# Loading the second feature tile's raw weights earlier and the first stored queries later in a fused linear-attention and gated-MLP layer

## The chip, the cores and the metric

The kernel runs on one core of one Trainium2 chip. The metric is the device time of one execution in microseconds (us). A profiled execution has a span (first to last instruction on the core) and, a little longer, its own time; both are given below.

## The reference

The layer normalises x (2048 tokens, 512 features) and runs two branches on the result.

```python
qkv = (xn @ wqkv) -> q, k, v                      # 32 heads of 16
pq, pk = q @ w_phi, k @ w_phi                     # per head
phi(p) = concat(softmax(p), softmax(-p))          # 32 features per head
kv = sum_s phi_k[s]^T v[s];  z = sum_s phi_k[s]
o  = (phi_q @ kv) / (phi_q . z + 1e-6)
s  = o @ wo
h  = relu(xn @ W_gate) * (xn @ W_up)              # 1376 features
g  = silu(h @ W_down)
out = x + s * g
```

All of it is float32.

## The kernel before, in words

**Arithmetic.** Every large float32 product is made of three matmuls on parts: a value is split into a high part, rounded on ScalarE (ACT), and a low part, the difference, on VectorE (DVE) or GpSimd (POOL). `mm3` (lines 204 to 213) issues low x high, high x low and high x high. Projections and the gate and up products use a seven-product scheme on two-by-two blocks (Strassen's kind): the token blocks and their sums lie in one resident tile `XT`, the weight blocks and their sums are prepared per tile of 128 features.

**Stages.** First come eight pairs of token tiles: normalise, transpose, project k and v, form the features `ek`, add their products with v into one accumulator `pkv`, and store the projected queries to DRAM (`pq...`). One column pair of the later queries is made by `q_tile` (lines 640 to 686) in the seven-product form, after the pairs. Then the feature tiles f = 0 to 10 run for the first half of the tokens, `gate_up_apart` (lines 757 to 805) while no down-projection is pending and `gate_up` afterwards, with `down` between them; then the output rows of that half; then the same for the second half with weights reloaded from DRAM.

**The first feature tiles.** `gate_up_apart` makes seven blocks of six matmuls in this order: pa (weights `wa`), pb and pc (`wb`), pd (`wc`), pa again (`wa`), pc again (`wc`), pd again (`wd`). Between them DVE combines the results: `u <- pb, t` (t is ACT's copy of pa, line 763), `e <- pc, u`, `e <- pd, e`, and so on. The second block on pc adds into the buffer that `e <- pc, u` reads, and the second block on pd adds into the buffer that `e <- pd, e` reads. So each of those two blocks waits for that DVE instruction.

**Preparation of a feature tile.** `f_load` (lines 535 to 544) issues three loads of 256 KB from SyncE's (SP's) queue: two halves of the raw gate and up weights, `rawg`, and the raw down weights, `rawd`. `f_prep` (lines 557 to 614) turns them into `wa`, `wb`, `wc`, `wd` and `fdh`, `fdl`: POOL forms the sums `tab`, ACT rounds, POOL subtracts, and each part is stored to DRAM (`ws...`) for the second half. At its end it calls `f_load` for the next tile (lines 607 to 612). The three raw tiles come from a pool of 40 buffers of 2 KB per partition, so a load waits until the earlier user of its buffer is done.

**State and queries.** `state` (lines 1426 to 1441) issues the last products into `pkv`, copies them (ACT, `kvacc`), transposes them (DVE, `kvT`) and copies the result into `kvt` (DVE, four copies). `normalizers` (lines 1443 to 1462) loads the second feature sum, `zodd`, for which SP waits until POOL's last accumulating transfer has landed. `q_load(u)` (lines 851 to 856) loads two stored query parts, `pql`. `q_pair(u)` (lines 858 to 952) transposes them on DVE (`pq <- pql`), takes the largest and smallest value per head (`mx`, two reductions), and shifts and exponentiates (`eq`).

**What sets the order.** Every engine runs its instructions in the order in which they are issued. A small clock model in the kernel (`Clock`, lines 68 to 161) holds generators such as `f_prep` and `q_pair`, each yielding the tiles that it wants next. At every `pump` the model decides by its own estimates whether a generator's next step is issued at that place. So a line that is moved can change the place of other steps too. Line 64 records every instruction, which is why all rows of the profile name it.

Of the kernel before, what the change touches and what calls it, by code (L numbers as in the profile page):

```python
# [20 lines left out]
NF = -(-F // P)  # L21
# [143 lines left out]
def layer_kernel(ctx: ExitStack, tc: tile.TileContext, x, wkT, wqT, wv, wo, wf, cst, out):  # L165
# [9 lines left out]
    def u8(shape, name, dt=F32):  # L175
        return sb.tile(list(shape), dt, tag="u8", bufs=B8, name=name)

    def u4(shape, name, dt=F32):
        return sb.tile(list(shape), dt, tag="u4", bufs=B4, name=name)

    def u2(shape, name, dt=F32):
        return sb.tile(list(shape), dt, tag="u2", bufs=B2, name=name)

    def small(n, name, bufs=3):
        return sb.tile([P, n], F32, tag=name, bufs=bufs, name=name)
# [4 lines left out]
    def f32(t):  # L190
        return t.bitcast(F32)

    def add(engine, o, a, b, op=ALU.add):
        engine.tensor_tensor(o, a, b, op=op)
# [23 lines left out]
    def flat(e):  # L218
        return e.rearrange("p h s f -> p (h s f)")
# [201 lines left out]
    def query(n):  # L421


        h, d = divmod(n, 4)
        if d // 2 in Q_TILES[h // 2]:
            return
        c = slice(h % 2 * 2 * P, (h % 2 + 1) * 2 * P)

        qs = [2 * b + h % 2 for b in PAIRS[h // 2][::-1]]
        p = ps((P, 2, 2 * P), name="pq")  # L430

        def w_of(d):
            return wq_part(d // 2, d % 2)
        if n < 2:
            i = 1 - n
            for d in range(2):
                mm3(p[:, d, :], w_of(d), lambda k: [XT[:, 2 * i + k // 2, s, k % 2, c] for s in range(2)], range(KD),
                    d == 0)
            to = [((qs[i], 0), slice(None), slice(None))]
        else:  # L440
            mm3(p, w_of(d), lambda k: [XT[:, k // 2:k // 2 + 3:2, s, k % 2, c] for s in range(2)], range(KD))
            to = [((q, d // 2), d % 2, i) for i, q in enumerate(qs)]
        t = u2((P, 2, 2 * P), "pqs")
        nc.scalar.activation(t, p, AF.Copy)
        for q, col, part in to:
            put_q(q, col, t, t[:, part, :])
# [78 lines left out]
    RAW, FT, WD = {}, {}, {}  # L525

    def two(name, apart):
        if apart:
            return [u2((P, 2, 2, P), name) for c in range(2)]
        t = u4((P, 2, 2, 2, P), name)  # L530
        return [t[:, c] for c in range(2)]
# [3 lines left out]
    def f_load(f):  # L535
        if f in AHEAD:

            t = u8((P, 2, 2, 2, 2, P), "rawg")
            RAW[f] = [t[:, 0, c] for c in range(2)], u2((P, D), "rawd"), [t[:, 1, c] for c in range(2)]
        else:  # L540
            RAW[f] = two("rawg", True), u2((P, D), "rawd"), None
        for c in range(2):
            nc.sync.dma_start(RAW[f][0][c].rearrange("p k s f -> p (k s f)"), wf[f][:, c * 512:(c + 1) * 512])
        nc.sync.dma_start(RAW[f][1], wf[f][:, 1024:])

    def w_pair(name):
        return u2((P, 2, 2, P), name, F32R), u2((P, 2, 2, P), name, F32R)
# [3 lines left out]
    def flat3(t):  # L551
        return t.rearrange("p a b c -> p (a b c)") if len(t.shape) > 2 else t

    def put(f, i, t):
        pace.when(t, lambda: nc.sync.dma_start(wspill[f][i], f32(flat3(t))))

    def f_prep(f, keep=True):


        rg, rd, tab = RAW.pop(f)  # L560
        b11, b12, b21, b22 = (rg[c][:, :, s, :] for c in range(2) for s in range(2))
        ta, tb = tab or two("tab", True)
        yield "gpsimd", b22
        add(nc.gpsimd, tb[:, 0], b12, b11, ALU.subtract)
        add(nc.gpsimd, ta[:, 1], b22, b12, ALU.subtract)
        if keep:
            wa, wb = w_pair("wa"), None
        else:
            t = u8((P, 4, 2, 2, P), "wab", F32R)
            wa, wb = (t[:, 0], t[:, 1]), (t[:, 2], t[:, 3])  # L570
        yield "scalar", b11
        for c in range(2):
            nc.scalar.activation(wa[0][:, c], rg[c][:, :, 0, :], AF.Copy)
        put(f, 0, wa[0])
        yield "gpsimd", ta
        add(nc.gpsimd, ta[:, 0], b22, tb[:, 0], ALU.subtract)
        add(nc.gpsimd, tb[:, 1], b21, ta[:, 0], ALU.subtract)
        wb = wb or w_pair("wb")
        yield "scalar", ta
        nc.scalar.activation(wb[0], ta, AF.Copy)  # L580
        put(f, 2, wb[0])
        for c in range(2):
            yield from sums_of(wa[1][:, c], rg[c][:, :, 0, :], f32(wa[0][:, c]), ALU.subtract, wa[0])
        put(f, 1, wa[1])
        wc = w_pair("wc")
        yield "scalar", tb
        nc.scalar.activation(wc[0], tb, AF.Copy)
        put(f, 4, wc[0])
        yield from sums_of(wb[1], ta, f32(wb[0]), ALU.subtract, wb[0])
        put(f, 3, wb[1])  # L590
        wd = u2((P, 2, 2, P), "wd", F32R)
        yield "scalar", b22
        nc.scalar.activation(wd[:, 0], b22, AF.Copy)
        yield from sums_of(wc[1], tb, f32(wc[0]), ALU.subtract, wc[0])
        put(f, 5, wc[1])
        fd = u2((P, D), "fdh", F32R), u2((P, D), "fdl", F32R)
        yield "scalar", rd
        nc.scalar.activation(fd[0], rd, AF.Copy)
        put(f, 7, fd[0])
        yield "gpsimd", wd  # L600
        add(nc.gpsimd, wd[:, 1], b22, f32(wd[:, 0]), ALU.subtract)
        put(f, 6, wd)
        yield from sums_of(fd[1], rd, f32(fd[0]), ALU.subtract, fd[0])
        put(f, 8, fd[1])
        if keep:
            FT[f], WD[f] = [wa, wb, wc, wd], fd
            nxt = f + 1
            while nxt in AHEAD:
                nxt += 1
            del rg, rd, ta, tb, tab  # L610
            if nxt < NF:
                f_load(nxt)
        DONE.add(f)
        yield None,
# [236 lines left out]
    def q_load(u):  # L851
        for j, part in enumerate(UNITS[u]):
            PQS[2 * u + j] = u2((P, 2, 2 * P), "pql")
            for g in PUT_Q.pop(part):
                pace.finish(g)
            nc.sync.dma_start(PQS[2 * u + j], PQ[part])
# [306 lines left out]
    def sums_of(o, a, b, op=ALU.subtract, *need):  # L1163

        yield "gpsimd", *(need or (a, b))
        add(nc.gpsimd, o, a, b, op)
# [252 lines left out]
    nc.vector.memset(ones, 1.0)  # L1419
    kvt = sb.tile([P, NG, 32], F32, tag="kvt", bufs=1, name="kvt")  # L1420
    nc.vector.memset(kvt, 0.0)
    q_load(0)
    query(N - 1)
    pace.pump()

# [17 lines left out]
    def normalizers():  # L1443
        nonlocal zB, zacc, zodd
        yield "sync", zacc2
        zodd = u4((P, H, 2, DH), "zodd")
        nc.sync.dma_start(flat(zodd), zacc2)
        yield 64,
        yield "tensor", zacc, zodd
        for part in (zacc, zodd):  # L1450
            z = flat(part).rearrange("p (a d i x) -> p i a d x", a=2, d=4, i=4)
            for i in range(4):
                r = slice(32 * i, 32 * i + 32)
                nc.tensor.matmul(PKV[0][r, 4:].rearrange("p (a b) (d x) -> p a (b d) x", a=2, x=32), ones, z[:, i],
                                 start=False, stop=True, skip_group_check=True, tile_position=(0, 32 * i))
        part = z = zacc = zodd = None
        t = small(256, "zB", 1).rearrange("p (d x) -> p d x", d=4)
        nc.scalar.activation(t.rearrange("p d (a x) -> p a d x", a=2),
                             PKV[0][:, 4:].rearrange("p (a b) (d x) -> p a (b d) x", a=2, x=32), AF.Copy)
        zB = t  # L1460
        PKV.clear()
        yield None,

    def all_queries(half):
        nonlocal zs
        if not half:
            yield from state()
            zs = pace.add(normalizers(), first=True)
            yield 24,
        for u, parts in enumerate(UNITS):  # L1470
            if parts[0][0] in QUERIES[half]:
                if u > 3:
                    yield "limit", (1.5, 1)
                yield from q_pair(u)
# [24 lines left out]
    for half in range(2):  # L1499
        b0, b1 = 2 * half, 2 * half + 1  # L1500
        if half == 0:
            queries = pace.add(all_queries(0), 30)
            at[0] = N
            for q in Q_TILES[1]:
                for _ in q_tile(1, q):
                    pace.pump()
# [126 lines left out]
```

## Time and profile before

| | before |
|---|---|
| time, median of 3 runs | 546.84 us (546.66 to 548.46) |
| the profiled execution's own time | 546.74 us |
| its span | 545.0 us, so 1.74 us lie around it |
| busy: PE (TensorE matmul) / PEld (its weight load) | 539.6 / 440.5 us |
| busy: DVE / ACT / POOL | 372.4 / 258.7 / 366.9 us |
| moved by DMA | 125.98 MB, mean 231 GB/s |

How to read the lines that follow. A row of the timeline gives the start in us from the span's start, the time taken, the engine, the line, the operation with its tiles (out <- in, buffer numbers left out), the shape and the count. Brackets give the idle time of that engine just before the row, and what seems to have ended it. A row on PEld shows a gap of TensorE that the PE row, whose ends are modelled, hides. A row of the windows gives the length of a stretch, then the busy time of each engine with its instruction count, the granted clock of TensorE as a share of full speed, the mean busy share of the 16 DMA engines and GB/s.

### The profile page before, as it was taken

How to read it: one execution, taken by the hardware profiler on the slowest of the kernel's cores; microseconds unless marked ns; L12 is line 12 of the kernel's file. 1: busy time of each engine (PE TensorE's matmuls, PEld its weight loads, DVE VectorE, ACT ScalarE, POOL GpSimd, SP SyncE). 2: the span in 40 equal slices, each digit the busy share in tenths (PEclk: the TensorE clock that was granted, in tenths of full speed). 3: DMA queues.
4: the chain of work that ended last, by engine and by line, in shares of the span. 5: the costliest groups of instructions: out<-in, count | busy, mean ns of one | idle time of the engine just before them, and what ended most of it. 6: DMA issues, size and time to landing. Idle time of an engine off the chain costs nothing.

```text
span 545.0 us, 9140 instructions
## 1 busy us (share of the span) xinstructions
PE 539.6 (99%) x3186; PEld 440.5 (81%) x3186; DVE 372.4 (68%) x585; ACT 258.7 (47%) x462; POOL 366.9 (67%) x328
## 2 busy tenths in 40 slices
PE   9999999999999999999999999999999999999997
PEld 8898888877887888787887888887777887878886
DVE  5988778677768338789883442899999494924323
ACT  3788767654435564545434240334354545342510
POOL 1569999767787999899896235262365765842591
PEclk9999999999999999999999999999999999999999
DMA  8339789555899957887869998692664735657073
GB/s 283 147 129 326 177 215 237 133 131 107 197 284 391 334 179 275 301 298 272 289 242 337 412 414 313 240 366 73 223 200 135 275 112 166 221 186 277 0 233 115
DMA packets 76367, 125.98 MB, mean 231 GB/s; under 512 B 6689, under 2 KB 29089, under 8 KB 75425
## 3 DMA queue, kind: packets, MB, share of 16 engines
q1 hardware_dynamic: 74160, 117.99, 61.7%
q0 software_dynamic: 2016, 7.34, 7.7%
q8 instruction: 25, 0.41, 0.3%
q14 instruction: 22, 0.17, 0.1%
q10 hardware_dynamic: 144, 0.07, 0.0%
HBM read 68.49 MB, written 52.69 MB: 222 GB/s over the span
## 4 chain that ended last, share of the span: by engine, by line
PE 90%; DVE 6%; issue 1%; DMA 1%; POOL 1%; ACT 0%; DVEq 0%; POOLq 0%; ACTq 0%
PE py L64 20%; PE pd L64 10%; PE pa L64 10%; PE pk L64 9%; PE pb L64 9%; PE pso L64 8%; PE pc L64 6%; PE pq L64 6%; PE pv L64 5%; PE pkv L64 2%; PE pfold L64 1%; PE pnum L64 1%; PE pxT L64 1%; DVE qs L64 1%; DMA wb<-ws 1%
## 5 line engine op out<-in xcount | busy, mean ns | idle before, releaser
L64 PE MATMUL py<-fdh,hl 128*128 128x512 f32 x176 | 69.1, 392 | 0.0
L64 PE MATMUL py<-fdl,hh 128*128 128x512 f32 x176 | 68.5, 389 | 0.0
L64 PE MATMUL py<-fdh,hh 128*128 128x512 f32 x176 | 68.5, 389 | 0.0
L64 PE MATMUL pa<-XT,wa 128*128 128x512 f32 x264 | 67.3, 390 | 0.0
L64 PEld LDWEIGHTS pa<-XT,wa 128*128 128x128 f32 x264 | 49.4, 188 | 11.1 <-POOL tab L64 0.4
L64 DVE TENSOR_TENSOR y<-py,y 128x512 f32<-128x512 f32 x40 | 27.5, 689 | 31.4 <-PE py L64 31.3
L64 POOL TENSOR_TENSOR hl<-t,hh 128x512 fp32r<-128x512 f32 x16 | 20.7, 1295 | 39.5 <-ACT hh L64 39.5
L64 POOL TENSOR_TENSOR y<-y,ys 128x512 f32<-128x512 f32 x24 | 30.9, 1292 | 17.9 <-ACT ys L64 17.4
L64 PEld LDWEIGHTS py<-fdh,hl 128*128 128x128 f32 x176 | 33.0, 188 | 8.8 <-issue 1.2
L64 PEld LDWEIGHTS py<-fdh,hh 128*128 128x128 f32 x176 | 33.0, 188 | 6.9
L64 POOL TENSOR_TENSOR ez<-eq,zB 128x1024 f32<-128x1024 f32 x16 | 38.5, 2412 | 0.1
L64 PEld LDWEIGHTS py<-fdl,hh 128*128 128x128 f32 x176 | 33.0, 188 | 6.7
L64 PE MATMUL pd<-XT,wd 128*128 128x512 f32 x132 | 33.9, 392 | 0.2
L64 PE MATMUL pd<-XT,wc 128*128 128x512 f32 x132 | 33.9, 391 | 0.0
L64 PE MATMUL pb<-XT,wb 128*128 128x512 f32 x132 | 33.6, 390 | 0.0
L64 POOL TENSOR_TENSOR ol<-of,oh 128x512 fp32r<-128x512 f32 (+1 forms) x13 | 19.8, 1548 | 20.3 <-ACT oh L64 20.3
L64 ACT ACTIVATE hh<-t 128x512 fp32r<-128x512 f32 x16 | 10.1, 633 | 49.3 <-DVE t L64 48.1
L64 PE MATMUL pc<-XT,wb 128*128 128x512 f32 x132 | 33.5, 389 | 0.0
L64 DVE TENSOR_REDUCE mx<-pk 128x32 f32<-128x512 f32 x32 | 20.5, 683 | 16.6 <-PE pk L64 16.5
L64 PE MATMUL pq<-XT,wqh 128*128 128x512 f32 (+1 forms) x112 | 30.6, 360 | 0.0
L64 DVE TENSOR_TENSOR pb<-pb,t 128x512 f32<-128x512 f32 x16 | 11.1, 696 | 28.4 <-ACT pd L64 28.3
L64 PE MATMUL pk<-wkh,XT 128*128 128x512 f32 x88 | 30.3, 396 | 0.0
(203 smaller groups left out, 1456.6 us busy)
## 6 DMA issues: line engine op xcount, KB each, us to landing
xts<-XT SPq DMA_DIRECT2D x4, 1792.0 KB
zacc<-ek POOLq DMA_DIRECT2D x14, 512.0 KB, 5.5
XT<-xts SPq DMA_DIRECT2D x7, 1024.0 KB
rawg<-wf SPq DMA_DIRECT2D x22, 256.0 KB
ws<-wa SPq DMA_DIRECT2D x22, 256.0 KB
ws<-wb SPq DMA_DIRECT2D x22, 256.0 KB
ws<-wc SPq DMA_DIRECT2D x22, 256.0 KB
wa<-ws SPq DMA_DIRECT2D x22, 256.0 KB
```

What stands on the lines that cost most here:

```text
L64: return self.tc.keep_in_program_order(op(*a, **k))
```

## The change

Three edits.

1. In `f_prep`, tile 0 calls `f_load(1)` right after its first two `wa` copies, where preparation begins, and no longer at its end.
2. At the end of `f_prep` the next tile is loaded only if it has not been loaded.
3. `q_load(0)`, the load of the first two stored query parts, moves from before the last query projection to `all_queries`, behind `state()` and the start of `normalizers`.

```diff
         for c in range(2):
             nc.scalar.activation(wa[0][:, c], rg[c][:, :, 0, :], AF.Copy)
         put(f, 0, wa[0])
+        if f == 0:
+            f_load(1)
         yield "gpsimd", ta
...
-            if nxt < NF:
+            if nxt < NF and nxt not in RAW:
                 f_load(nxt)
...
     nc.vector.memset(kvt, 0.0)
-    q_load(0)
     query(N - 1)
...
             yield from state()
             zs = pace.add(normalizers(), first=True)
+            q_load(0)
             yield 24,
```

**SP, from the end of the pairs to the first feature tile.** The piece below is of the difference (minus: before, plus: after). `pql` are the first query parts, `rawg` and `rawd` the raw weights of tile 1, `ws_..._71` to `_75` stores of tile 0's parts, `ws_0_77` the first store of tile 1's.

```order
+L64 DMA ws_3_71<-wb 128x512
+L64 DMA ws_7_75<-fdh 128x512
+L64 DMA ws_5_73<-wc 128x512
+L64 DMA ws_0_77<-wa 128x512
 L64 DMA pql<-pq_1414 128x512
 L64 DMA pql<-pq_1731 128x512
-L64 DMA ws_3_71<-wb 128x512
-L64 DMA ws_7_75<-fdh 128x512
-L64 DMA rawg<-wf 128x512 x2
-L64 DMA rawd<-wf 128x512
-L64 DMA ws_5_73<-wc 128x512
 L64 DMA ws_6_74<-wd 128x512
```

The query loads now stand behind four stores, the last of which belongs to tile 1. The loads of tile 1 are gone from here: they now directly follow the loads of tile 0, ahead of a store of projected queries (`pq_1730 <- pqs`).

**ACT, from the q tile to the first block of tile 0.** `t_1912` and `t_2058` (before) are the copies of pa in the q tile and in tile 0; `wa`, `wb`, `wc`, `wd`, `fdh` here are tile 1's. Before:

```order
L64 ACTIVATE t_1912<-pa 128x512 x2
L64 ACTIVATE wa<-rawg 128x256 x2
L64 ACTIVATE kvacc<-pkv 128x256
L64 ACTIVATE wb<-tab 128x512
L64 ACTIVATE wc<-tab 128x512
L64 ACTIVATE wd<-rawg 128x256
L64 ACTIVATE fdh<-rawd 128x512
L64 ACTIVATE t_2058<-pa 128x512
```

After:

```order
L64 ACTIVATE t_1914<-pa 128x512
L64 ACTIVATE wa<-rawg 128x256 x2
L64 ACTIVATE t_1914<-pa 128x512
L64 ACTIVATE kvacc<-pkv 128x256
L64 ACTIVATE wb<-tab 128x512
L64 ACTIVATE wc<-tab 128x512
L64 ACTIVATE wd<-rawg 128x256
L64 ACTIVATE fdh<-rawd 128x512
L64 ACTIVATE t_2058<-pa 128x512
```

The two `wa` copies of tile 1, which need the raw weights, moved ahead of the second copy of the q tile; what follows `kvacc` stands as it did.

**DVE, from the end of the q tile to the first queries.** `u_1923`, `e_1942`, `t_2015` are the q tile's sums, `u_2078` and `e_2092` those of feature tile 0, `pq_2095` and `mx` the first query part. Before:

```order
L64 TENSOR_TENSOR t_2015<-pc,u_1923 128x512
L64 STREAM_TRANSPOSE kvT<-kvacc 128x256
L64 COPY kvt<-kvT 32x8x16 x4
L64 TENSOR_TENSOR u_1923<-pd,u_1923 128x512
L64 TENSOR_TENSOR u_2078<-pb,t_2058 128x512
L64 TENSOR_TENSOR e_2092<-pc,u_2078 128x512
L64 STREAM_TRANSPOSE pq_2095<-pql 128x512
L64 TENSOR_REDUCE mx<-pq_2095 128x32 x2
L64 TENSOR_TENSOR e_2092<-pd,e_2092 128x512
```

After:

```order
L64 STREAM_TRANSPOSE kvT<-kvacc 128x256
L64 COPY kvt<-kvT 32x8x16 x4
L64 TENSOR_TENSOR t_2022<-pc,u_1925 128x512
L64 TENSOR_TENSOR u_1925<-pd,u_1925 128x512
L64 TENSOR_TENSOR u_2078<-pb,t_2058 128x512
L64 STREAM_TRANSPOSE pq_2088<-pql 128x512
L64 TENSOR_REDUCE mx<-pq_2088 128x32 x2
L64 TENSOR_TENSOR e_2098<-pc,u_2078 128x512
L64 TENSOR_TENSOR e_2098<-pd,e_2098 128x512
```

Two things moved: the state's transpose and copies went ahead of one sum of the q tile, and the first query's transpose and reductions went ahead of `e <- pc, u` of tile 0. The order on PE is the same in both kernels, and POOL's too.

## The prediction

> **What bounds the kernel now.** I read the page first, then TensorE's gaps on its weight loads, then what each gap waited for.
>
> ```profile
> span 545.0 us, 9140 instructions
> PE 539.6 (99%) x3186; PEld 440.5 (81%) x3186; DVE 372.4 (68%) x585; ACT 258.7 (47%) x462; POOL 366.9 (67%) x328
> PEclk9999999999999999999999999999999999999999
> PE 90%; DVE 6%; issue 1%; DMA 1%; POOL 1%; ACT 0%; DVEq 0%; POOLq 0%; ACTq 0%
> ```
>
> TensorE (PE) is busy for 99% of the span at full clock, and 90% of the chain that ended last is its own work. The change leaves its 3186 matmuls in their order. So the only time to be had, or lost, lies in PE's waits. In the stretch that the change touches, from 130 us to 185 us, the weight loads show two gaps that are not part of a fixed sequence and that the moved steps can reach:
>
> ```profile
> 162.10 1.32 PEld L64 LDWEIGHTS pc<-XT,wc 128*128 128x128 f32 x6
> 163.84 1.22 PEld L64 LDWEIGHTS pd<-XT,wd 128*128 128x128 f32 x6 [0.43 <-POOL fdl L64]
> ...
> 179.63 0.19 PEld L64 LDWEIGHTS py<-fdh,hl 128*128 128x128 f32 x1 [0.35 <-POOL hl L64]
> ```
>
> The matmul rows around them give what each gap cost:
>
> ```profile
> 160.96 1.52 PE L64 MATMUL pa<-XT,wa 128*128 128x512 f32 x6
> 162.32 1.52 PE L64 MATMUL pc<-XT,wc 128*128 128x512 f32 x6
> 163.88 1.63 PE L64 MATMUL pd<-XT,wd 128*128 128x512 f32 x6
> 165.34 0.85 PE L64 MATMUL pa<-XT,wa 128*128 128x512 f32 x3
> ...
> 178.86 0.39 PE L64 MATMUL py<-fdh,hl 128*128 128x512 f32 x1
> ...
> 180.43 1.54 PE L64 MATMUL pb<-XT,wb 128*128 128x512 f32 x6
> ```
>
> Blocks of six start 162.32 - 160.96 = 1.36 us apart. After pc at 162.32 the pa block should start at 162.32 + 2 x 1.36 = 165.04; it starts at 165.34. **Gap 1 costs 0.30 us.** After py at 178.86 the next block should start at 180.22; it starts at 180.43. **Gap 2 costs 0.21 us.** Together 0.51 us, or 0.09% of the time.
>
> **What gap 1 waited for.** The row names POOL's fdl, but pd's second block adds into the buffer that DVE's `e <- pd, e` reads.
>
> ```profile
> 157.70 0.69 DVE L64 TENSOR_TENSOR u<-pd,u 128x512 f32<-128x512 f32 x1
> 159.69 0.69 DVE L64 TENSOR_TENSOR u<-pb,t 128x512 f32<-128x512 f32 x1 [1.29 <-ACT t L64]
> 160.48 0.69 DVE L64 TENSOR_TENSOR e<-pc,u 128x512 f32<-128x512 f32 x1
> 161.09 0.72 DVE L64 STREAM_TRANSPOSE pq<-pql 128x512 f32<-128x512 f32 x1
> 161.84 1.29 DVE L64 TENSOR_REDUCE mx<-pq 128x32 f32<-128x512 f32 x2
> 163.05 0.68 DVE L64 TENSOR_TENSOR e<-pd,e 128x512 f32<-128x512 f32 x1
> ```
>
> It ends at 163.05 + 0.68 = 163.73, and the load starts 0.11 us later. It was late because the chain began late: `u <- pb, t` waited 1.29 us for ACT's t.
>
> ```profile
> 154.68 0.42 ACT L64 ACTIVATE wa<-rawg 128x256 fp32r<-128x256 f32 x1 [2.33 <-DMA rawg<-wf]
> 155.59 0.37 ACT L64 ACTIVATE kvacc<-pkv 128x256 f32<-128x256 f32 x1
> 156.84 0.63 ACT L64 ACTIVATE wb<-tab 128x512 fp32r<-128x512 f32 x1 [0.88 <-POOL tab L64]
> 159.02 0.58 ACT L64 ACTIVATE t<-pa 128x512 f32<-128x512 f32 x1
> ...
> 151.41 1.04 POOL L64 TENSOR_TENSOR wd<-rawg,wd 128x256 fp32r<-128x256 f32 x1
> 152.11 1.58 POOL L64 TENSOR_TENSOR fdl<-rawd,fdh 128x512 fp32r<-128x512 f32 x1
> 154.66 1.44 POOL L64 TENSOR_TENSOR tab<-rawg 128x256 f32<-128x256 f32 x2 [0.98 <-DMA rawg<-wf]
> ...
> 149.11 1.64 SPq L64 DMA_DIRECT2D rawg<-wf  x2
> ```
>
> Tile 1's raw weights were issued at 149.11 and had not landed before about 154.6; ACT stood still 2.33 us for them and POOL 0.98 us. From POOL's `tab` to ACT's t the distance is 159.02 - 154.66 = 4.36 us, all of it tile 1's preparation.
>
> **Edit 1 and 2, the early load.** It removes the wait for the raw weights. POOL's `tab` then follows fdl directly: at 152.11 + 1.58 = 153.69 if fdl's shown length counts. In the rows, though, wd has 1.04 shown and fdl still starts 0.70 after it, and later
>
> ```profile
> 177.02 1.31 POOL L64 TENSOR_TENSOR fdl<-rawd,fdh 128x512 fp32r<-128x512 f32 x1
> 178.27 1.31 POOL L64 TENSOR_TENSOR hl<-e,hh 128x512 fp32r<-128x512 f32 x1
> ```
>
> an fdl's follower starts 1.25 after it, which makes 153.36. So `tab` starts between 153.36 and 153.69, and t between 157.72 and 158.05. (The pa block ends near 157.04, four block distances and a tail of 0.16 from the rows above, so t is not held back.) t ends 0.58 later and `u <- pb, t` follows 0.09 later, as before (159.60 to 159.69): **158.39 to 158.72**, where it was 159.69. By then DVE is free: kvacc no longer stands behind the stalled wa, so it runs between 152.35 (154.68 - 2.33) and 154.68. The q tile's last sum ended 157.70 + 0.69 - 155.59 = 2.80 after kvacc's start, and with the one sum that now stands behind kvT it is 3.4, so it ends by 158.1 at the latest.
>
> The Trainium skill, "Perfetto Trace Analysis", section GPSIMD Instruction, says that a POOL instruction's span is unreliable and that such instructions are timed from start to start. By that rule the early end of each bound above holds, and by the shown spans the late one; wd's 0.70 against 1.04 sides with the rule.
>
> **The moved queries (edit 3 and the reordering).** In DVE's new order the transpose and the two reductions stand ahead of `e <- pc, u`. With the distances of the rows (0.61, 0.75, 1.21) it starts 2.57 after u and ends 3.26 after it: 161.65 to 161.98. The pc block that waits for it wants its load at 162.10, and the load comes 0.11 after the release: 161.76 to 162.09. It fits, with 0.01 to 0.34 us to spare. `e <- pd, e` ends 0.6 later, by 162.57, a full 0.9 before pd's load is wanted (163.46). **Gap 1 goes: -0.30 us**, between -0.30 and about -0.2 if the pc block has to wait a little.
>
> **Gap 2** is the first down-projection waiting for `hl`, the last of a POOL row of work without a break:
>
> ```profile
> 164.84 0.69 DVE L64 TENSOR_TENSOR pc<-pc,u 128x512 f32<-128x512 f32 x1
> 165.57 0.69 DVE L64 SCALAR_TENSOR_TENSOR e<-pc,e 128x512 f32<-128x512 f32 x1
> ...
> 166.29 0.63 ACT L64 ACTIVATE hh<-e 128x512 fp32r<-128x512 f32 x1 [6.69 <-DVE e L64]
> 167.79 0.70 ACT L64 ACTIVATE wa<-rawg 128x256 fp32r<-128x256 f32 x2
> ...
> 167.00 1.31 POOL L64 TENSOR_TENSOR hl<-e,hh 128x512 fp32r<-128x512 f32 x1 [3.54 <-ACT hh L64]
> ...
> 162.11 1.04 SPq L64 DMA_DIRECT2D rawg<-wf  x2
> ```
>
> From 167.00 to the `hl` at 178.27 POOL never stops. `pc <- pc, u` is then held by PE alone, whose pc block ends at 162.32 + 1.52 = 163.84; with 0.04 it starts at 163.88 where it started at 164.84, so this row comes 0.96 earlier. What can hold it is tile 2's raw load. That landed by 167.79 at the latest (ACT's wa shows no wait); POOL wants it at 168.31 - 0.96 = 167.35. If it lands no earlier than that latest bound the gain is 0.5, else 0.96. To close gap 2, with PE itself 0.30 earlier, `hl` must come 0.21 + 0.30 = 0.51 earlier. **Gap 2: -0.21 us**, or about nothing less at the low end.
>
> **Costed at nothing.** Tile 1's three loads are now issued ahead of a query store:
>
> ```profile
> 129.80 1.28 POOL L64 TENSOR_TENSOR XT<-xf,XT 128x512 fp32r<-128x512 f32 x1
> ...
> 132.71 0.80 SPq L64 DMA_DIRECT2D pq<-pqs  x2
> ...
> 124.00:134.00 10.00, 9.87 (x104) 7.84 (x103) 9.23 (x15) 5.95 (x10) 6.58 (x8) 1.00 0.38 67
> 150.00:156.00 6.00, 6.00 (x87) 4.79 (x86) 3.22 (x8) 1.71 (x4) 4.22 (x5) 1.00 1.03 284
> ```
>
> Their buffers were last used by sums that POOL finishes at 131.08, so SP issues them at about 131.1 to 133.2 (two took 1.64), and the store at 132.71 may slip by 0.5. Its first reader is the pql load, more than 10 us later. The 0.75 MB leave a stretch in which the DMA engines are full (1.03) for one where they are at 0.38. The pql loads go behind `ws_0_77 <- wa`, whose copy now follows the first t of the q tile; they are issued by about 149.5. A raw load issued from 149.11 had landed by 154.68, so pql is there some 4 us before DVE wants it at about 159. Without that cover each us late would cost PE a us.
>
> **The sum.** 546.74 (the profiled execution's own time) - 0.30 - 0.21 = **546.2 us**; against the median of 546.84 this is the same difference, since the two lie 0.1 apart.
>
> **Rivals.**
>
> *Slower: the queries in the way.* If the t chain does not come earlier (POOL's fdl or the raw load as late as before), the new DVE order itself costs. u at 159.69 gives `e <- pc, u` an end at 159.69 + 3.26 = 162.95, pc's load at 163.06 instead of 162.10: 0.96 lost for the 0.30 of today. That is +0.66, **547.4 us**. It decides where u starts later than 162.10 - 0.11 - 3.26 = 158.73. For it: my late bound is 158.72, so there is hardly any room. Against: POOL's start-to-start times, and that ACT no longer stands still. Chance 0.15.
>
> *Nothing gained.* The wait at 154.68 is not the only thing between POOL's fdl and PE; if half of the 0.97 us is lost again and tile 2's load lands as late as today, gap 1 turns into an equal wait of pc and gap 2 stays: **546.7 us**, within 0.2. The change would then not do what it says: the load is early, but nobody is ready earlier. Chance 0.18.
>
> *pql or a buffer late.* If tile 1's load is held until its old place, wa, its store and both pql loads move to 156 or later, and by the landing time of a raw load (150.75 to about 155) DVE would stall until 160.5 or beyond: e <- pc, u ends at 163.15 or later, PE loses 1.1 us or more in place of 0.30: **547.6 us and up**. For it only that SP is one queue; against it the free buffers at 131. With several us of delay it passes 0.3%. Chance 0.07, counted whole as over 0.3%.
>
> **How the numbers follow.** The forecast, a gain of 0.3 to 0.6, has 0.53; a larger gain than the two gaps, from waits further on that I cannot see, 0.07. 0.3% is 1.64 us, about what a measurement of this kernel can tell from no change. The forecast, the slower rival and the case without gain all lie inside it: 0.53 + 0.15 + 0.18 = 0.86; with 0.07 and 0.07 outside. The range of 545.6 to 547.6 runs from the forecast less the scatter of the runs to the late-query rival.
>
> **What would show it.** Right: no DMA wait ahead of ACT's `wa <- rawg` near 148; `tab` at about 153.5, t at about 158, no gap ahead of pd's wd block, none at the py block near 179, and blocks after 181 half a us earlier. Wrong: a gap ahead of the second pc block near 162 with DVE's `e <- pc, u` just before it; a wait of DVE for pql; or gaps after 185 that before did not have, since I hold that stretch for unchanged.

## The result, and the profile after

The changed kernel takes **546.20 us** (median of 20 executions, 545.94 to 547.74) where the kernel before took 547.33 (20 executions, 546.37 to 549.0). The ratio is 0.9982, with a 95% interval of 0.9974 to 0.999, so 0.5 to 1.4 us less. That lies inside the 0.3% that counted as no change here, though the interval does not contain 1. The profiled execution has an own time of 546.34 and a span of 544.5 us, against 546.74 and 545.0. Single executions of 617 us and more occurred with several kernels, the one before among them: two profiles of the kernel before fell on such and are not used, and three of the medians below contain one, which moves them by less than 0.02 us.

The page's line of busy times, then TensorE's timeline around the two gaps:

```profile
PE 539.1 (99%) x3186; PEld 440.8 (81%) x3186; DVE 372.5 (68%) x585; ACT 258.6 (47%) x462; POOL 366.7 (67%) x328
```

```profile
161.10 1.52 PE L64 MATMUL pa<-XT,wa 128*128 128x512 f32 x6
162.46 1.52 PE L64 MATMUL pc<-XT,wc 128*128 128x512 f32 x6
163.82 1.52 PE L64 MATMUL pd<-XT,wd 128*128 128x512 f32 x6
165.18 1.07 PE L64 MATMUL pa<-XT,wa 128*128 128x512 f32 x4
...
178.69 0.39 PE L64 MATMUL py<-fdh,hl 128*128 128x512 f32 x1
...
180.05 1.52 PE L64 MATMUL pb<-XT,wb 128*128 128x512 f32 x6
```

Every step is now 1.36 us: both gaps are gone. In this execution PE's blocks run 0.14 us later from the first stages on (161.10 for 160.96). The change has no part in that: it goes back to a weight load at 9.51 us that waited 0.29 us for the transfer of `wkT`, more than 100 us ahead of the first step that moved. Rows of the two kernels are compared less these 0.14 us.

The chain behind gap 1, in DVE's, ACT's and POOL's timelines:

```profile
158.77 0.69 DVE L64 TENSOR_TENSOR u<-pb,t 128x512 f32<-128x512 f32 x1 [2.20 <-ACT t L64]
159.38 0.72 DVE L64 STREAM_TRANSPOSE pq<-pql 128x512 f32<-128x512 f32 x1
...
161.34 0.68 DVE L64 TENSOR_TENSOR e<-pc,u 128x512 f32<-128x512 f32 x1
162.12 0.69 DVE L64 TENSOR_TENSOR e<-pd,e 128x512 f32<-128x512 f32 x1
```

```profile
147.69 0.71 ACT L64 ACTIVATE wa<-rawg 128x256 fp32r<-128x256 f32 x2
...
152.95 0.38 ACT L64 ACTIVATE kvacc<-pkv 128x256 f32<-128x256 f32 x1 [0.46 <-PE pkv L64]
155.91 0.63 ACT L64 ACTIVATE wb<-tab 128x512 fp32r<-128x512 f32 x1 [2.57 <-POOL tab L64]
158.10 0.58 ACT L64 ACTIVATE t<-pa 128x512 f32<-128x512 f32 x1
```

```profile
152.24 1.57 POOL L64 TENSOR_TENSOR fdl<-rawd,fdh 128x512 fp32r<-128x512 f32 x1
153.47 1.71 POOL L64 TENSOR_TENSOR tab<-rawg 128x256 f32<-128x256 f32 x2
154.86 1.84 POOL L64 TENSOR_TENSOR tab<-rawg,tab 128x256 f32<-128x256 f32 x2
166.19 1.29 POOL L64 TENSOR_TENSOR hl<-e,hh 128x512 fp32r<-128x512 f32 x1 [3.65 <-ACT hh L64]
```

Nobody waits for `rawg` any more: `wa` runs at 147.69, long before ACT needs it, and `tab` follows fdl at once. The bracket on `u <- pb, t` shows 2.20 us of idle DVE; it is no loss, since DVE was done with the q tile's sums earlier (the last starts at 155.88, for 157.70 before), and the block that needs `e <- pc, u` gets it in time.

SP's timeline:

```profile
130.00 1.58 SPq L64 DMA_DIRECT2D rawg<-wf  x2
132.86 0.81 SPq L64 DMA_DIRECT2D pq<-pqs  x2
149.10 1.20 SPq L64 DMA_DIRECT2D pql<-pq  x2
```

The load now goes out at 130.00. In the two stretches of the windows that the prediction quoted, the share of the DMA engines rises from 0.38 to 0.60 (124 to 134 us) and falls from 1.03 to 0.98 (150 to 156 us), and PE's busy time in the first is the same 9.87.

### The profile page after: what moved, and what is told of

It is laid out like the page before. It is cut to its first block, busy times and chain, and to the rows that moved or that the text cites. A ratio compares the mean times of both kernels' runs of the same rounds, so it can differ in the third digit from the quotient of the medians.

```text
span 544.5 us, 9142 instructions
## 1 busy us (share of the span) xinstructions
PE 539.1 (99%) x3186; PEld 440.8 (81%) x3186; DVE 372.5 (68%) x585; ACT 258.6 (47%) x462; POOL 366.7 (67%) x328
## 4 chain that ended last, share of the span: by engine, by line
PE 89%; DVE 6%; issue 1%; DMA 1%; POOL 1%; ACT 0%; SPq 0%; DVEq 0%; POOLq 0%; ACTq 0%
PE py L64 20%; PE pd L64 10%; PE pa L64 10%; PE pk L64 9%; PE pb L64 9%; PE pso L64 8%; PE pc L64 7%; PE pq L64 6%; PE pv L64 5%; PE pkv L64 2%; PE pnum L64 1%; PE pxT L64 1%; DMA wkT<-wkT 1%; DVE qs L64 1%; PE pfold L64 1%
```

## The experiments

**Theory:** tile 1's raw weights land just in time in the kernel before; the landing sets ACT's `t` and so gaps 1 and 2, us for us. **Rivals:** the new orders on ACT and DVE do it by themselves; or the spread between executions, which is as large as the gain, has another cause.

### One half of the change at a time

The early load alone (edits 1 and 2):

```diff
         put(f, 0, wa[0])
+        if f == 0:
+            f_load(1)
...
-            if nxt < NF:
+            if nxt < NF and nxt not in RAW:
```

> Edits 1 and 2 alone (tile 1's raw weights early, the first queries loaded at their old place). The compute engines then have the changed kernel's whole order, so the reordering on DVE and ACT comes from the early load and not from edit 3. Theory A (the change is worth its two TensorE gaps, 0.51 us, and what the medians show beyond that is scatter between executions): both gaps gone, raw-load wait gone, span 0.4 to 0.5 us below before. Theory B (before, the raw load lands so late that its landing time varies from execution to execution and each us costs; the early load also removes that): the same gaps gone, and a median about 1 us below before with its high executions gone. Rival (edit 3 is needed, because the query loads otherwise come in the way): one of the two gaps stays, gain 0.3 us or less.

546.20 us, ratio 0.9984 (0.9974 to 0.9993). Both gaps are gone, as TensorE's timeline shows by the step of 1.36 from one block to the next:

```profile
164.09 1.52 PE L64 MATMUL pd<-XT,wd 128*128 128x512 f32 x6
165.45 0.84 PE L64 MATMUL pa<-XT,wa 128*128 128x512 f32 x3
```

The order on ACT and DVE is already that of the full change. So the reordering comes from edits 1 and 2, not from the moved query load.

The later query load alone (edit 3):

```diff
-    q_load(0)
     query(N - 1)
...
             zs = pace.add(normalizers(), first=True)
+            q_load(0)
```

> Edit 3 alone. The engines' order stays that of before; SP issues tile 1's loads ahead of the two query loads and so about 2 to 3 us earlier, near 146 us instead of 149. If a landing before about 152 us is all that matters, POOL's tab follows fdl without a wait, the q-tile and feature-tile copies on ACT come about 1 us earlier and both gaps close: gain 0.3 to 0.5 us, the same as the whole change. If the new order on ACT and DVE is what closes the gaps, gap 1 stays near 0.4 us of idle weight load and the gain is below 0.15 us. Theory B expects the high executions of before to become fewer but not to go, since the load still lands within some us of its need.

546.36 us, ratio 0.9989 (0.998 to 0.9997). Here ACT, DVE and POOL keep the order of before, and yet both gaps are gone. TensorE's timeline:

```profile
163.54 1.52 PE L64 MATMUL pd<-XT,wd 128*128 128x512 f32 x6
164.90 1.30 PE L64 MATMUL pa<-XT,wa 128*128 128x512 f32 x5
```

The reason is on SP. Its timeline in this kernel:

```profile
144.17 0.40 SPq L64 DMA_DIRECT2D ws<-wb  x1
...
145.16 0.92 SPq L64 DMA_DIRECT2D rawg<-wf  x2
```

and the same place in the kernel before, with a row of SP's waits there (columns: who waited, for what; us in total, times, longest):

```profile
144.31 2.78 SPq L64 DMA_DIRECT2D pql<-pq  x2
147.18 1.21 SPq L64 DMA_DIRECT2D ws<-wb  x1
...
SPq L64 <- DMA pq<-pqs: 2.0, 1, 2.0
```

In the kernel before SP stood still 2.0 us at the second query load, until the store of the very part that it reads had landed, and the `ws <- wb` store behind it took 1.21 us to issue for 0.40 here. Everything queued behind, the raw weights among it, went out 4 us later: 149.11 for 145.16. Four us are enough; ACT's `wa` at 152.10 then waits for nothing. So either half of the change closes both gaps, by different ways, and the two together bring no more than one.

### The new order without the early load

The full change's orders on PE, ACT, DVE and POOL with edits 1 and 2; only the three transfers themselves are issued where the kernel before issues them (the clock model is told of them early, and they are sent late).

```diff
-            f_load(1)
+            f_load(1, send=False)
...
-            if nxt < NF and nxt not in RAW:
-                f_load(nxt)
+            if nxt < NF:
+                f_load(nxt, tell=nxt not in RAW)
```

> The engines' order of the changed kernel, but tile 1's raw loads issued at their old place on SP (near 149 us); the query loads at their old place too. This is the slower rival of the prediction made real: the first query's transpose and reductions stand ahead of e<-pc,u, and ACT's t is as late as before. Expected from the prediction: e<-pc,u ends near 162.95, a gap of about 1.0 us ahead of the second pc block, gap 1 replaced, time 0.66 us above before (547.4 us against a profiled 546.74), and gap 2 as before or larger. If instead the time stays within 0.2 us of before, DVE's order has more room than the rows say.

547.15 us, ratio 1.0001 (0.9992 to 1.001): no gain. TensorE's timeline has one gap, at another block:

```profile
161.01 1.52 PE L64 MATMUL pa<-XT,wa 128*128 128x512 f32 x6
163.35 1.65 PE L64 MATMUL pc<-XT,wc 128*128 128x512 f32 x6 [0.82 <-DVE e L64]
...
166.22 1.52 PE L64 MATMUL pa<-XT,wa 128*128 128x512 f32 x6
```

166.22 - 161.01 - 3 x 1.36 = 1.13 us are lost, ahead of pc, and none at py. That is the slower rival of the prediction, at the place and in the way that it named; against the 0.51 of before it is 0.62 dearer in the profile (0.66 was worked out), 547.35 against 546.74. That the two sizes agree so well is luck: pc lost 1.13 us where the rival had 0.96, because `t` came 0.37 us later still than in the profile of before (159.39) and `u` started at 160.05 for 159.69; and the 0.21 at py, which the rival left standing, went, because TensorE arrived there 0.87 us later. In the medians a loss is not shown: the interval reaches about half a us either way. The new order brings no gain by itself; it asks for the early weights.

The same with edit 3 as well, that is the whole change with only the transfers late:

> The changed kernel with tile 1's three raw transfers issued where the kernel before issues them (behind ws_7_75), all else in the changed order: so wa, its store ws_0_77 and both query loads behind it wait too. This is the rival of the prediction with a late query load. The order alone with a late load cost PE 1.13 us at the pc block. By the rival's working the query loads go out at about 156, land 2 to 5 us later, and DVE's transpose waits: e <- pc, u ends at 163.2 or later, PE loses 1.1 us or more in place of 0.5, and the time is 547.5 or above, up to 550. If the query loads are covered even then (landing before about 160.7), it equals the late load with the changed order: 547.2, ratio 1.000.

546.35 us, ratio 0.9984 (0.9976 to 0.9993), no gap: the dear rival did not happen. SP's, ACT's and DVE's timelines:

```profile
145.41 0.91 SPq L550 DMA_DIRECT2D rawg<-wf  x2
152.81 1.68 SPq L64 DMA_DIRECT2D pql<-pq  x2
...
151.95 0.42 ACT L64 ACTIVATE wa<-rawg 128x256 fp32r<-128x256 f32 x1 [2.78 <-DMA rawg<-wf]
152.27 0.58 ACT L64 ACTIVATE t<-pa 128x512 f32<-128x512 f32 x1
...
159.26 0.72 DVE L64 STREAM_TRANSPOSE pq<-pql 128x512 f32<-128x512 f32 x1
```

With the query loads behind them, the raw weights go out at 145.41 though nothing was done to send them early; in the kernel just above, with the query loads ahead, it was 149.15. The second half lands by 151.95, which holds the q tile's `t` on ACT (152.27) by half a us and costs TensorE nothing. The query load, issued at 152.81, is there when DVE transposes at 159.26, without a wait. The only difference between these two kernels is the place of two query loads on SP, and it is worth the 1.13 us gap.

### A dose: the load later still

The kernel before with four small transfers on SP just ahead of tile 1's raw load:

```diff
+        if f == 1:
+            for k in range(4):
+                nc.sync.dma_start(dram((1, 1024), f"pad{k}"), wf[f][k:k + 1, :1024])
         for c in range(2):
             nc.sync.dma_start(RAW[f][0][c]...
```

> The kernel before with four small transfers of 4 KB (a row of the weights, copied to an unused place in DRAM) put on SP's queue directly ahead of tile 1's raw load; the order on every other engine is that of before. At about 0.4 us of issue each the raw load goes out about 1.6 us later. Theory (the raw weights land just in time in the kernel before, so each us that they are later costs PE a us): the wait of ACT's wa grows from 2.3 to about 3.9 us, the gap ahead of pd's wd block at 163.8 from 0.3 to about 1.9 us of lost time (a part of it may appear as a gap of pc), and the median goes from 547.0 to about 548.6. Rival (the load is not what sets the time, and the spread of the runs of before has another cause): within 0.3 us of before.

550.69 us, ratio 1.0065 (1.0053 to 1.0077): 3.5 us slower. The dose was larger than meant. The four transfers took 2.64 us to issue, not 1.6, and the weights landed later by more. ACT's second copy `wa` shows when the second half is there. SP's, ACT's and TensorE's timelines:

```profile
150.05 2.64 SPq L64 DMA_DIRECT2D pad<-wf  x4
...
158.78 0.42 ACT L64 ACTIVATE wa<-rawg 128x256 fp32r<-128x256 f32 x1 [5.65 <-DMA rawg<-wf]
160.07 0.42 ACT L64 ACTIVATE wa<-rawg 128x256 fp32r<-128x256 f32 x1 [0.87 <-DMA rawg<-wf]
163.82 0.58 ACT L64 ACTIVATE t<-pa 128x512 f32<-128x512 f32 x1
...
160.39 1.52 PE L64 MATMUL pd<-XT,wc 128*128 128x512 f32 x6
164.44 1.85 PE L64 MATMUL pa<-XT,wa 128*128 128x512 f32 x6 [2.53 <-ACT t L64]
...
170.34 1.52 PE L64 MATMUL pa<-XT,wa 128*128 128x512 f32 x6
```

and the second `wa` in the kernel before:

```profile
155.26 0.42 ACT L64 ACTIVATE wa<-rawg 128x256 fp32r<-128x256 f32 x1 [0.17 <-DMA rawg<-wf]
```

Without a gap the pa block would start at 160.39 + 1.36 = 161.75 and the next pa at 165.83; it starts at 170.34, so 4.51 us are lost. `t` comes 163.82 - 161.75 = 2.07 us after the time at which that pa block is due; in the kernel before it came 1.94 before it (159.02 against 160.96), for a cost of 0.30. So `t` is 4.01 us later and the cost 4.21 larger: about one us for one. The second `wa` starts 161.75 - 160.07 = 1.68 us before that time, and 160.96 - 155.26 = 5.70 before it in the kernel before, so the weights are 4.02 us later, which is what `t` is. The profiled execution, 551.32, is the slowest of the five, so it loses more than the medians.

### The kernel before, profiled again

The kernel as it was, four times, to see what moves between executions. The first, beside the halves:

> The kernel before, unchanged. Shows how far a ratio of two identical kernels strays and whether its executions scatter as widely as those of before (546.4 to 549.0 us). Theory A and B both expect a ratio of 1.000 within 0.05% and both gaps (0.43 and 0.35 us of idle weight load) in its profile; theory B expects the raw load's landing, the start of ACT's wa, to differ by some tenths of a us or more from the first profile.

The other three, for their profiles:

> The kernel before, unchanged, for a second profiled execution. Theory (the spread between executions of before is the landing time of tile 1's raw weights): if its own time differs from 546.74, then the wait of ACT's wa differs from 2.33 us by about as much in the same direction, and the blocks up to 160 us do not. Rival (spread from elsewhere): own time and the wait for the raw weights are unrelated, and gaps 1 and 2 cost 0.30 and 0.21 again whatever the time. Ratio 1.000 within 0.001.

> The kernel before, a third profiled execution. Theory: the cost of gap 1 (start of the pa block near 165.3, less the start of pc, less 2.72) follows ACT's kvacc, which stands behind the second wa, us for us: kvacc 155.59 and gap 1 0.30 in the first profile, kvacc 0.21 earlier against the blocks and gap 1 0.10 in the second. Rival: gap 1 does not follow it.

> The kernel before, a fourth profiled execution, for the same reading as the third: kvacc's start against the d block of tile 0 (159.60 in the first profile) and the costs of gaps 1 and 2, against its own time.

The unchanged kernel had medians of 547.02 and 547.00 (ratios 0.9998 and 1.0002, both with 1 in the interval); the two profiles used had own times of 546.62 and 546.80. ACT's and TensorE's timelines, of the kernel with own time 546.62:

```profile
155.18 0.42 ACT L64 ACTIVATE wa<-rawg 128x256 fp32r<-128x256 f32 x1 [0.44 <-DMA rawg<-wf]
158.94 0.58 ACT L64 ACTIVATE t<-pa 128x512 f32<-128x512 f32 x1
...
161.08 1.52 PE L64 MATMUL pa<-XT,wa 128*128 128x512 f32 x6
165.26 1.52 PE L64 MATMUL pa<-XT,wa 128*128 128x512 f32 x6
```

and of the one with 546.80:

```profile
155.29 0.42 ACT L64 ACTIVATE wa<-rawg 128x256 fp32r<-128x256 f32 x1 [0.30 <-DMA rawg<-wf]
159.07 0.58 ACT L64 ACTIVATE t<-pa 128x512 f32<-128x512 f32 x1
...
161.38 1.52 PE L64 MATMUL pa<-XT,wa 128*128 128x512 f32 x6
165.48 1.52 PE L64 MATMUL pa<-XT,wa 128*128 128x512 f32 x6
```

| kernel, execution | second `wa` before the pa block is due | `t` before it is due | cost of gap 1 |
|---|---|---|---|
| before with the four transfers | 1.68 us | -2.07 us | 4.51 us |
| before, the prediction's profile | 5.70 | 1.94 | 0.30 |
| before, second | 5.90 | 2.14 | 0.10 |
| before, third | 6.09 | 2.31 | 0.02 |
| after | over 13 | 3.00 | 0 |

While the weights are late, `t` starts 3.75 to 3.78 us after the second `wa`, and gap 1 follows the landing in the same kernel from one execution to the next: 0.20 us earlier, 0.20 less. Gap 2 shrank as well in these three, to 0.19 and 0.11 from 0.21 (from the py block to the next, less 1.36), but not us for us. Own time is not settled by it alone: the third had gap 1 at 0.02 and yet 546.80, because its blocks run 0.42 us later from the first stages on (161.38 for 160.96), so the first transfers of the program spread the times too.

### The change a second time

> The changed kernel, unchanged, a second time and with a second profile. Both theories: median 546.2, ratio to before 0.998. Theory (landing of tile 1's raw weights is what spreads the times of before): its executions lie within about 0.6 us of each other (546.0 to 546.6), apart from one in ten, and no gap stands ahead of the pc and pd blocks near 163 nor at py near 179. Rival (the spread has another cause, common to both kernels): a spread of 2 us as before has.

546.35 us, ratio 0.9986 (0.9977 to 0.9996), no gap in its profile; 7 of 10 executions lie below 546.5, three between 546.7 and 547.3, a little more spread than expected. Over all comparisons, the five runs whose raw weights land by 152 us (the change twice, each half, and the change with late transfers) have 61 executions with a median of 546.24; 50 are below 546.5 and 6 above 547. The kernel before has 121, with a median of 547.07; 12 are below 546.5 and 65 above 547. The fastest executions of the two groups lie close together, 545.94 and 546.08; it is the slower ones that go.

### Further versions

The gap at 134 us that no part of the change touches: ACT's copy of `pk` stands behind tile 0's `wa` copies. One line more lets the preparation wait:

```diff
+        if f == 0:
+            yield 4,
         yield "scalar", b11
         for c in range(2):
             nc.scalar.activation(wa[0][:, c], rg[c][:, :, 0, :], AF.Copy)
```

> The changed kernel with one line more: tile 0's preparation waits for four token blocks of the clock model before its first ACT copies, so that the copy of pk in the last pair stands ahead of tile 0's two wa copies on ACT (nothing else moves). The gap of the weight load at 133.99 (0.56 idle, ended by ACT's pk) costs PE 133.99 - (133.47 + 0.23) = 0.29 us. Theory: pk's copy ends 0.6 us earlier, the gap goes, wa is 0.6 us later without anybody waiting: 0.3 us less than the changed kernel, 545.9 median, ratio to before about 0.998. Rival: POOL's row or the stores behind wa come later and give it back at the first blocks of tile 0: 546.2, or a gap near 163.

545.83 us, ratio 0.9975 (0.9966 to 0.9984). ACT's timeline has the two exchanged, and TensorE's weight load comes without a bracket:

```profile
132.42 0.59 ACT L64 ACTIVATE pk<-pk 128x512 f32<-128x512 f32 x1
132.94 0.71 ACT L64 ACTIVATE wa<-rawg 128x256 fp32r<-128x256 f32 x2
...
133.16 0.19 PEld L64 LDWEIGHTS pk<-h,XT 128*128 128x128 f32 x1
```

It is 0.4 to 0.5 us under the changed kernel, where 0.29 was expected. On top of it, less backlog for the query steps of the second half:

```diff
                 if u > 3:
-                    yield "limit", (1.5, 1)
+                    yield "limit", (0.75, 1)
```

> The kernel with pk's copy first (545.83 median, 1.4 us under before), and the query steps of the second half allowed half as much of a backlog on DVE (limit 0.75 for 1.5), so that the sum t <- pd, t no longer stands behind the two reductions mx. In the changed kernel that sum holds TensorE at 373.02 and 389.67, 0.41 and 0.53 us. Theory (the sum is late only because it is queued behind query work): both gaps go and nothing else is late, 544.9. Rival (the query work is only pushed back and is late at the end of the half, or the query products then cut into the gate and up blocks at other places): the gaps reappear elsewhere, 545.5 to 546.5.

545.19 us (544.88 to 545.4), ratio 0.9961 (0.9948 to 0.9975): the fastest version, 0.6 us under the one before it where 0.9 was worked out. DVE's timeline shows the sum ahead of the reductions:

```profile
371.19 0.67 DVE L64 TENSOR_TENSOR t<-pd,t 128x512 f32<-128x512 f32 x1
371.78 1.27 DVE L64 TENSOR_REDUCE mx<-pq 128x32 f32<-128x512 f32 x2
```

Both gaps of the sum are gone. Where the other 0.3 went was not followed up.

## Why the prediction was right, and where it was not

**Gap 1, 0.30, and gap 2, 0.21.** Both went, so the sum of 0.51 is what this profile lost: 0.40 in own time and 0.14 given back by the late first stages.

**The early load.** Right in kind and in time. Less the 0.14, `tab` starts at 153.33, t at 157.96, u at 158.63, and `e <- pc, u` ends at 161.88; the ranges were 153.36 to 153.69, 157.72 to 158.05, 158.39 to 158.72 and 161.65 to 161.98. `tab` came at the early bound, though from `tab` to t it took 4.63 us and not the 4.36 carried over, so t came near the late one. The 4.36 is the term that was off here, by 0.27; the last section shows where that lies. The rule of the Trainium skill, "Perfetto Trace Analysis", section GPSIMD Engine Instruction, to time POOL from start to start, gave `tab`'s start (1.23 after fdl's, whose shown length is 1.57). When a reader gets the result has to be read elsewhere, as the last section shows.

**"The moved queries (edit 3 and the reordering)".** This step failed in what it credited. The order on DVE and ACT is the work of edits 1 and 2; edit 3 acts on SP alone. The prediction quoted the issue at 149.11 and did not ask what SP had done before it. The query loads were costed at nothing as a step that moves late; that they had held the raw weights for 4 us where they stood was missed, and so was that edit 3 would have sufficed. The number is not touched by it, because two ways to the same early landing do not add.

**Gap 2.** `hl` came 0.81 earlier by the rows and 0.95 with the 0.14 taken off, where 0.96 (at least 0.5) was forecast; tile 2's raw load was no limit. `pc <- pc, u` started at 163.89 with the 0.14 taken off, for 163.88, which agrees with PE's pc block holding it.

**Costed at nothing.** Right, with one reading wrong: the raw load went out at 130.00 and not from 131.1, so the sums that POOL finishes at 131.08 did not hold its buffers. The store behind the early load went out at 132.86 for 132.71, which the late first stages explain, and the query loads went out at 149.10 (by 149.5 was forecast).

**"Against the median of 546.84 this is the same difference".** This is the term that was mis-sized. Medians differ by 1.1 us here, 0.5 to 1.4 by the interval, not 0.51. That the median of the changed kernel is the forecast's 546.2 to the digit is partly luck: the forecast starts from one execution of before that lies 0.6 under that kernel's median of 547.33, and the medians differ by more than this execution's two gaps. The profiled execution of before was not typical: all three that were profiled have own times of 546.62 to 546.80, below the median of 547.07 of the 121. In the kernel before each us of later landing costs PE about one (the dose), and the landing varies; with the early load it has some us to spare. That this is what makes the executions of 547 to 549 us is an inference from the dose, the table and the two spreads. No execution of before between 547 and 549 us was profiled, and the first stages spread the times as well.

**The rivals.** The slower one was real but not chosen: its condition, u later than 158.73, was missed by 0.10 (158.63 with the 0.14 taken off), and in the late-weights version it held (160.05). The one with late queries was priced from a query load held until 156; with the transfers at their old place the weights move up in SP's queue, to 145.41, the query loads go out at 152.81, and it costs nothing. The case without gain did not occur.

## What to carry to other kernels

When a load is late, read its own queue backwards from its issue: an entry ahead that waits for something else holds everything behind it, and moving that entry can be worth as much as moving the load. Where a wait ends just in time, the cost in one profile is one draw; take several executions, and the gain in the median can be larger than the gap that a good execution shows. A new order that a scheduler derives from an earlier load can cost more than the old one if the data is late after all (0.62 us in one profile here), so test the order and the load apart.

## What the runs showed of the hardware that was not expected

**On POOL the start and the shown end time different things.** `tab`'s two instructions are shown with 1.44 us in all behind an idle POOL (before) and with 1.71 directly behind fdl (after), the next two with 1.55 and 1.84. ACT's `wb`, which reads them, starts 156.84 - 154.66 = 2.18 us after `tab`'s start in the one case and 155.91 - 153.47 = 2.44 in the other. Standing directly behind another instruction is not the reason: tile 2's `tab`, directly behind `hl`, is shown with 1.44 in both kernels, and `wb` follows its start by 2.17 (168.26 to 170.43 before, 167.45 to 169.62 after). The long rows come behind the issue of the accumulating transfer `zacc` on POOL at 150.9 (after): wd has 1.03 there for 0.74 later, fdl 1.57 for 1.30. In that stretch each row starts 0.32 to 0.34 before its predecessor's shown end, in the later rows 0.03 to 0.05. What makes them long was not tested. The distance from start to start tells when the next row begins, but a reader follows the shown end: ACT's `wc`, which also waited for `tab`, starts 0.04 after the end of the second `tab` pair in both kernels (156.70 and 156.74 after, 157.62 and 157.66 before), and TensorE's load of `hl` in the prediction 0.05 after `hl`'s (179.58 and 179.63).

**Issue times on SP differ with what is around.** One store took 1.21 us to issue in the kernel before and 0.40 with the query loads out of the way; four transfers of 4 KB took 0.66 each, though 0.4 had been read from larger ones. No run varied the cause of either alone.
